# An earlier last conversion, smaller attention buffers and two more prefetched weight quarters

## The chip, the cores and the metric

The kernel runs on one core of one Trainium2 chip. The metric is the device time of one execution in microseconds (us). Three runs of the kernel before took 621.95, 622.92 and 623.33 us, so the median is 622.92 us. The profiled execution took 622.67 us, of which 620.7 us lie between its first and its last instruction.

## What is computed

Three layers follow one another, all in float32 precision; the last layer's two weight matrices arrive as float64 words, which the kernel converts to float32 on the chip.

```python
# attention: 4 batches x 12 heads, 448 positions, head size 64
scores = cap * tanh(q @ k.T / sqrt(64) / cap)
x = (exp(scores - max) / (sum + 1e-9)) @ v             # -> x: 1792 tokens x 768

# soft mixture of 8 experts with 4 slots each
logits = x @ phi                                       # 1792 x 32
slot_in = softmax_over_tokens(logits).T @ x            # 32 x 768
for e in range(8):                                     # each expert sees its own 4 slots
    slot_out[e] = relu(slot_in[e] @ w1[e]) @ w2[e]     # w1: 768x1024, w2: 1024x768
x = softmax_over_slots(logits) @ slot_out

# MLP: w_in 768x2048, w_out 2048x768
h = x @ w_in
out = (max(h, 0) + alpha * min(h, 0)) @ w_out
```

## The kernel before

**Attention.** Two heads make a pair, and there are 24 pairs. One loop runs over steps g; pair i has the four steps 4i to 4i+3. The keys of a pair are cut into four chunks that are taken in the order 0, 3, 1, 2. Chunks 0, 1 and 2 hold 128 keys of both heads, so their tile P is 128 x 896 numbers; chunk 3 is the last-key tile: the remaining 64 keys of both heads, 128 x 448 numbers. In a step `qk` (line 365) issues the score matmuls of one chunk, then ScalarE (ACT) takes tanh (line 380) and exp (line 381) of them into a tile P. Two steps later `pv` (line 384) multiplies that tile with v. GpSimd (POOL) adds the P tiles into `acc`: at chunk 1 the sum of chunks 0 and 1 (line 396) and the two halves of the last-key tile (line 400, two instructions), at chunk 2 the third chunk (line 403). Two steps after that, `row_sums` (line 409, tile `rs`) sums `acc` over the keys with TensorE (PE). In the last pair only line 396 runs on POOL, and `row_sums` is called directly in the last step and reads the other tiles itself.

P has four buffers for all chunks, and `acc` two: one for even pairs (pool `acc0`) and one for odd pairs (pool `acc1`). PE's instructions in attention are chained in the written order (line 281); the other engines' order comes from a scheduler that takes the written order and swaps neighbours by its own estimate of when each is ready. Each engine then runs its queue in order.

**Conversion of w_in in the background.** w_in comes in 24 pieces. `conv_w_in` (lines 667 and 176 to 191) turns one piece into float32: one ACT instruction (abs, line 178) and four VectorE (DVE) instructions (lines 179, 183, 186, 189). `store_w_in`, two steps later, writes it to memory and loads the piece after next. `cv_at` (line 663) gives the step of piece n: 4, 6, then 4n+1, so the second step of each pair; the last is step 93, in pair 23. The pieces pass through `cvbuf`, which is slot 10 of the weight slots; it is freed with the last store, at step 95.

**Weights.** There are eleven weight slots of 1.57 MB (`NA`), and expert weights come in halves of that size: w1 of expert 0 in two, w2 in two, and so on. During attention `LOADS` (line 55) names the pairs at whose fourth step the next half is loaded, if a slot is free; the ten slots 0 to 9 are loaded in the pairs 2 to 20, slot 10 in pair 23. Of the twelfth half one quarter (393 KB) is loaded ahead (`load_early`, line 116, `QE` = 1) in pair 21. After attention seven more slots (`NX`) lie in the memory that the attention pools leave; they are loaded in 27 quarters, in address order (line 111), and each waits for the attention tiles under it. All loads go through one queue, SP's, in order. The pools lie one behind the other in the order of lines 232 to 246: nat0, nat1 (4096 bytes a partition each), stk0 (7680), vn0 (1792), acc0 (3584), stk1 (7680), pt (14336) and on. The first quarters therefore lie over nat0, nat1 and stk0, the sixth and seventh reach into acc0.

**Experts and MLP.** PE goes through the eight experts (w1, then w2); when a half has been used, its slot takes the next load (`done_with`, line 171). The MLP follows on the same queue with the converted w_in and with w_out.

Of the kernel before, what the change touches and what calls it, by code (L numbers as in the profile page):

```python
# [8 lines left out]
F32 = mybir.dt.float32  # L9
# [15 lines left out]
def tile_attention_soft_moe_mlp(ctx, tc, q, k, v, cap, phi, w1, w2, w_in, w_out, alpha, out):  # L25
    nc = tc.nc
    B, H, S, D = q.shape
    J = 4
# [4 lines left out]
    NSLOT = phi.shape[1]  # L33
# [8 lines left out]
    SLOT = 3072  # L42
    NA = 11
    NX = 7
    QE = 1
    JK = 3
    KEYS = 128 * JK
    TAIL = S - KEYS
# [3 lines left out]
    LAG = 2  # L52

    CHUNKS = (0, 3, 1, 2)
    LOADS = (2, 4, 6, 8, 10, 12, 14, 16, 18, 20, 22, 23)

    EH = 5
    TBS = (4, 2, 2, 2, 2, 2)
# [16 lines left out]
    xslots = []  # L75
    early = [arena.tile([128, SLOT // 4], F32, tag=f"early{c}", name="w") for c in range(QE)]

# [19 lines left out]
    def may_load():  # L97
        if nload[0] == len(loads):
            return None
        late = loads[nload[0]][0] in ("wi", "wo")  # L100
        fit = [n for n in free if not late or n < NA]
        return fit[0] if len(fit) > (late and kept[0] < NWO) else None
# [124 lines left out]
    def attention():  # L227
        with ExitStack() as pools:
            def pool(name, bufs=1, **kw):
                return pools.enter_context(tc.tile_pool(name=name, bufs=bufs, **kw))  # L230

            nat_0 = pool("nat0")
            nat_1 = pool("nat1")
            stk_0 = pool("stk0")
            v_0 = pool("vn0")
            acc_0 = pool("acc0")
            stk_1 = pool("stk1")
            pt_p = pool("pt", 4)
            v_1 = pool("vn1")
            acc_1 = pool("acc1")  # L240
            ac0_p = pool("aconst0")
            xn_p = pool("xn", 7)
            xu_p = pool("xu", 4)
# [1 line left out]
            sm_p = pool("sm")  # L245
# [2 lines left out]
            ps_a = pool("ps_a", 3, space=PSUM)  # L248
            ps_o = pool("ps_o", space=PSUM)

            nat_p, stk_p, v_p, acc_p = (nat_0, nat_1), (stk_0, stk_1), (v_0, v_1), (acc_0, acc_1)
            stackI = ac_p.tile([128, 128], F32, name="stackI")
            sel = ac0_p.tile([128, GP, 2, 2, 64], F32R, name="sel")
            hot = ac0_p.tile([128, 64], F32, name="hot")
# [3 lines left out]
            phi_rep = ac_p.tile([128, 128], F32, name="phi_rep")  # L258
            z_run = ac_p.tile([128, 1], F32, name="z_run")

            def head(u):
                return slice(64 * u, 64 * u + 64)
# [6 lines left out]
            nat, stk, sc_t, pt, acc, ov, xu, xn = {}, {}, {}, {}, {}, {}, {}, {}  # L269
# [7 lines left out]
            def matmul(*a, **kw):  # L277
                ins = nc.tensor.matmul(*a, **kw)  # L278
                if order:
                    if order[0] is not None:  # L280
                        tc.add_manual_dep(ins.ins, order[0].ins.name, NOSYNC, reason="tilings together")
                    order[0] = ins
                return ins
# [5 lines left out]
            def later(d, fn, *a):  # L289
                bg.setdefault(now[0] + d, []).append((fn, a))  # L290
# [74 lines left out]
            def qk(i, c):  # L365

                kh, kl = stk["k", i]
                qh, ql = stk["q", i]
                ps = ps_s.tile([128, 2, 512], F32, tag="s", name="s")
                for n, (a, b) in enumerate(((kh, qh), (kh, ql), (kl, qh))):  # L370
                    flags = dict(start=(n == 0), stop=(n == 2))
                    if c == JK:
                        matmul(ps[:, 0, :S], a[:, KEYS:], b, **flags)
                        continue
                    for u in range(2):
                        o = 128 * c
                        matmul(ps[:, u, :S], a[head(u), o:o + 128], b[head(u)], **flags)
                n = 1 if c == JK else 2
                pe = pt_p.tile([128, n, S], F32, tag="p", name="p")
                nc.scalar.activation(out=pe, in_=ps[:, :n, :S], func=AF.Tanh)  # L380
                nc.scalar.activation(out=pe, in_=pe, func=AF.Exp, scale=cap_sb)  # L381
                pt[i, c] = pe

            def pv(i, c):
                if c == 0:
                    ov[i] = ps_o.tile([128, 512], F32, tag="o", name="o")
                    acc[i] = acc_p[i % 2].tile([128, 2, S], F32, tag="acc", name="acc")
                o, a, t, pe = ov[i], acc[i], nat["v", i], pt[i, c]
                if i == NPAIR - 1 and c == 2:
                    row_sums(i)  # L390
                for u in range(2):
                    r = slice(TAIL * u, TAIL * u + TAIL)
                    lhsT, rhs = (t[r, 2 * JK, :], pe[r, 0, :]) if c == JK else (t[:, JK * u + c, :], pe[:, u, :])
                    matmul(o[64 * u:64 * u + 64, :S], lhsT, rhs, start=(c == 0), stop=(c == 2))
                if c == 1:
                    nc.gpsimd.tensor_add(out=a, in0=pt[i, 0], in1=pe)  # L396
                    for u in range(2):
                        r = slice(TAIL * u, TAIL * u + TAIL)
                        if i < NPAIR - 1:
                            nc.gpsimd.tensor_add(out=a[r, u, :], in0=a[r, u, :], in1=pt[i, JK][r, 0, :])  # L400
                if c == 2:
                    if i < NPAIR - 1:
                        nc.gpsimd.tensor_add(out=a, in0=a, in1=pe)  # L403
                    xu[i] = xu_p.tile([128, J * 128], F32, tag="xu", name="xu")[:, :S]
                    nc.scalar.activation(out=xu[i], in_=o[:, :S], func=AF.Copy)  # L405
                    if i < NPAIR - 1:
                        later(2, row_sums, i)
# [252 lines left out]

            ncv = KD * (DFF // 512)

            def cv_at(n):

                return J + 2 * n if n < 2 else J * n + 1

            def conv_w_in(i):
                fb, kk = divmod(i, KD)
                t = cvbuf[:, 2, i % 2 * 512:i % 2 * 512 + 512].bitcast(F32)
                to_f32(craw.pop(i), t, (order[0], latest[0]))  # L670
                cout[i] = t
# [30 lines left out]
            for g in range(NPAIR * J + LAG):  # L702
                now[0] = g
                i, c = divmod(g, J)
# [4 lines left out]
                if i < NPAIR:  # L709
                    qk(i, CHUNKS[c])  # L710
                    if c == 1 and i + 1 < NPAIR:
                        trans_k(i + 1)
                        trans_q(i + 1)
                run_bg()
                if i < NPAIR:
                    if c == 0:
                        last = load(i + 2, "kq") or last
                    if c == 2:
                        if i == NPAIR - LAG - 1:
                            load_early(last)  # L720
                    if g == 2:
                        load_w_in(0)
                        load_w_in(1)
                    for n in range(ncv):
                        if cv_at(n) == g - 2:
                            store_w_in(n)
                        if cv_at(n) == g:
                            conv_w_in(n)
                    if c == 3 and i in LOADS and may_load() is not None:
                        load_next(last)  # L730
                if g >= LAG:
                    n, e = divmod(g - LAG, J)
                    pv(n, CHUNKS[e])
                    if e == J - 1:
                        load(n + 2, "v")
# [4 lines left out]

            nc.vector.tensor_scalar(out=z_run, in0=z_run, scalar1=1e-9, scalar2=None, op0=ALU.add)
            nc.vector.reciprocal(out=z_run, in_=z_run)
            diag = sm_p.tile([128, NSLOT], F32, tag="diag", name="diag")
            nc.vector.tensor_scalar(
                out=diag, in0=stackI[:, 0:NSLOT], scalar1=z_run, scalar2=None, op0=ALU.mult
            )
# [10 lines left out]
    def tail():  # L757
# [254 lines left out]
        with (  # L1012
# [3 lines left out]
            with tc.tile_pool(name="ex2", bufs=1, reuse_waits="tile", side="right") as ex2_p:  # L1016
# [6 lines left out]
                with (  # L1023
# [9 lines left out]
                    mlp(ps_w, ps_c, ex_p, cv_p, g_p, ob_p, so, cstk)  # L1033

    attention()
    tail()

# [29 lines left out]
```

## Time and profile before

| | kernel before |
|---|---|
| median of three runs | 622.92 us |
| profiled execution | 622.67 us |
| span of its instructions | 620.7 us |
| attention, to its last matmul | 0 to 274.2 us |
| experts on PE | 274.2 to 349.3 us |
| MLP | 349.3 us to the end |
| busy: PE / DVE / ACT / POOL | 578.6 / 394.7 / 319.3 / 160.1 us |
| moved by DMA | 110.9 MB |

A share of busy time is an average over these three stages, which have different limits, so each stage is read by itself: its waits, and what ends them.

### The profile page before, as it was taken

The numbers are of one execution on the slowest core, as the hardware profiler recorded it, in microseconds if no ns is written. First come the engines' busy times: TensorE is split into PE (matmuls) and PEld (weight loads), VectorE is DVE, ScalarE is ACT, GpSimd is POOL, SyncE is SP. The second block draws the span as 40 slices with busy tenths as digits, with TensorE's granted clock in tenths as the row PEclk, the third lists the DMA queues.
The fourth block names the chain that finished last, engine by engine and source line by source line (L and its number), as shares of the span: only waits on it lengthen the run. The fifth ranks groups of instructions, "written<-read, shape, count | busy, mean of one in ns | idle before, by whom it ended". The sixth has DMA issues, their size and how long they took to land.

```text
span 620.7 us, 10735 instructions
## 1 busy us (share of the span) xinstructions
PE 578.6 (93%) x4110; PEld 384.7 (62%) x4110; DVE 394.7 (64%) x734; ACT 319.3 (51%) x509; POOL 160.1 (26%) x111
## 2 busy tenths in 40 slices
PE   6799898999999999989896899999999999999996
PEld 4344344455445445454452568888888888888886
DVE  4568667696769879640013399999566666666662
ACT  4798898888889687420101266764412121121211
POOL 0668668475848457100000000000000000000000
PEclk9899999999999999979998899999999999999999
DMA  4786897887978661599999999200301001010101
GB/s 103 199 260 158 260 265 214 261 213 210 262 227 265 207 171 53 194 373 370 403 404 407 389 402 408 102 1 1 103 1 51 1 21 32 0 52 2 51 1 51
DMA packets 95169, 110.90 MB, mean 179 GB/s; under 512 B 56208, under 2 KB 70032, under 8 KB 95120
## 3 DMA queue, kind: packets, MB, share of 16 engines
q1 hardware_dynamic: 94976, 110.24, 55.0%
q8 instruction: 32, 0.52, 0.3%
q14 instruction: 17, 0.14, 0.1%
q10 hardware_dynamic: 144, 0.00, 0.0%
HBM read 98.41 MB, written 11.80 MB: 178 GB/s over the span
## 4 chain that ended last, share of the span: by engine, by line
PE 64%; DMA 15%; DVE 8%; ACT 7%; POOL 3%; issue 1%; SPq 1%; ACTq 0%; POOLq 0%
PE oc L941 13%; PE oc L947 13%; PE oc L948 13%; DMA w<-in_moe_w_dram 12%; PE o L278 6%; PE s L278 5%; ACT p L381 2%; PE hps L896 2%; PE aps L870 2%; ACT p L380 2%; DMA q<-in_q_dram 2%; POOL acc L400 2%; PE rs L278 1%; DMA cvbuf<-in_moe_w_in_dram 1%; PE nx L278 1%
## 5 line engine op out<-in xcount | busy, mean ns | idle before, releaser
L947 PE MATMUL oc<-wsp,gh 128*128 128x512 f32 x448 | 151.7, 339 | 0.0
L941 PE MATMUL oc<-wsp,gh 128*128 128x512 f32 x448 | 151.6, 338 | 0.0
L948 PE MATMUL oc<-wsp,gl 128*128 128x512 f32 x448 | 150.7, 337 | 0.0
L912 ACT ACTIVATE gh<-gf 128x256 fp32r<-128x256 f32 (+1 forms) x96 | 43.5, 453 | 133.0 <-DVE gf L911 127.1
L278 PE MATMUL o<-p,v 128*64 128x448 f32 (+1 forms) x384 | 94.0, 568 | 10.1 <-ACT xu L405 10.0
L380 ACT ACTIVATE p<-s 128x896 f32<-128x896 f32 x96 | 79.0, 824 | 28.6 <-PE s L278 19.7
L381 ACT ACTIVATE p<-p,cap 128x896 f32<-128x896 f32 x96 | 91.2, 951 | 2.3
L941 PEld LDWEIGHTS oc<-wsp,gh 128*128 128x128 f32 x448 | 85.0, 190 | 10.7 <-issue 0.9
L948 PEld LDWEIGHTS oc<-wsp,gl 128*128 128x128 f32 x448 | 84.7, 189 | 11.1 <-issue 1.2
L947 PEld LDWEIGHTS oc<-wsp,gh 128*128 128x128 f32 x448 | 85.0, 190 | 9.7 <-issue 0.4
L913 DVE TENSOR_TENSOR gl<-gf,gh 128x256 fp32r<-128x256 f32 (+1 forms) x96 | 45.0, 469 | 45.3 <-ACT gh L912 45.2
L396 POOL TENSOR_TENSOR acc<-p 128x896 f32<-128x896 f32 x24 | 53.0, 2207 | 77.8 <-ACT p L381 77.8
L278 PEld LDWEIGHTS s<-qh,kh 64*128 64x128 f32 (+1 forms) x168 | 18.1, 186 | 67.1 <-ACT p L380 26.1
L400 POOL TENSOR_TENSOR acc<-acc,p 64x448 f32<-64x448 f32 x46 | 54.3, 1180 | 3.1
L908 DVE TENSOR_SCALAR mn<-hps,alpha 128x256 f32<-128x256 f32 (+1 forms) x81 | 39.5, 487 | 23.6 <-PE hps L896 23.5
L403 POOL TENSOR_TENSOR acc<-acc,p 128x896 f32<-128x896 f32 x23 | 49.0, 2129 | 1.8
L278 PE MATMUL s<-qh,kh 64*128 64x448 f32 (+1 forms) x168 | 45.8, 475 | 0.0
L278 PEld LDWEIGHTS o<-p,v 128*64 128x64 f32 (+1 forms) x384 | 19.0, 134 | 34.8 <-ACT xu L405 16.4
L911 DVE SCALAR_TENSOR_TENSOR gf<-hps,mn 128x256 f32<-128x256 f32 (+1 forms) x81 | 34.6, 427 | 2.7
L278 PE MATMUL s<-qh,kl 64*128 64x448 f32 (+1 forms) x168 | 35.5, 367 | 0.0
L278 PE MATMUL s<-ql,kh 64*128 64x448 f32 (+1 forms) x168 | 35.3, 365 | 0.0
L810 PE MATMUL h<-w,slotT 128*32 128x256 f32 x384 | 30.6, 418 | 4.5 <-DMA w<-in_moe_w_dram 4.5
(151 smaller groups left out, 771.6 us busy)
## 6 DMA issues: line engine op xcount, KB each, us to landing
w<-in_moe_w_dram SPq DMA_DIRECT2D x80, 384.0 KB, 8.4
w<-in_moe_w_dram SPq DMA_DIRECT2D x36, 512.0 KB, 8.2
cvbuf<-in_moe_w_in_dram SPq DMA_DIRECT2D x24, 512.0 KB, 4.5
w<-in_moe_w_out_dram SPq DMA_DIRECT2D x16, 768.0 KB, 8.9
w_in<-cvbuf SPq DMA_DIRECT2D x24, 256.0 KB, 2.4
q<-in_q_dram SPq DMA_DIRECT2D x48, 112.0 KB, 4.0
k<-in_k_dram SPq DMA_DIRECT2D x48, 96.0 KB, 5.1
v<-in_v_dram SPq DMA_DIRECT2D x24, 192.0 KB, 3.4
```

The costliest lines, as they stand in the source:

```text
L278: ins = nc.tensor.matmul(*a, **kw)
L380: nc.scalar.activation(out=pe, in_=ps[:, :n, :S], func=AF.Tanh)
L381: nc.scalar.activation(out=pe, in_=pe, func=AF.Exp, scale=cap_sb)
L396: nc.gpsimd.tensor_add(out=a, in0=pt[i, 0], in1=pe)
L400: nc.gpsimd.tensor_add(out=a[r, u, :], in0=a[r, u, :], in1=pt[i, JK][r, 0, :])
L403: nc.gpsimd.tensor_add(out=a, in0=a, in1=pe)
L908: nc.vector.tensor_scalar(out=mn, in0=ps, scalar1=0.0, scalar2=alpha_sb[:, f:f + 1], op0=ALU.min, op1=ALU.mult)
L912: nc.scalar.activation(out=gh, in_=gf, func=AF.Copy)
L913: nc.vector.tensor_sub(out=gl, in0=gf, in1=gh)
L941: ins = nc.tensor.matmul(o, gh[:, ts], wo_h[f][:, cols], start=(f == 0 and not second), stop=False)
L947: nc.tensor.matmul(o, gh[:, ts], wo_l[f][:, cols], start=False, stop=False)
L948: nc.tensor.matmul(o, gl[:, ts], wo_h[f][:, cols], start=False, stop=(f == KF - 1 and not more))
```

## The change

The last piece of w_in is converted at step 85 (pair 21) and not 93. For that the first fourteen pieces come at steps that are mostly three apart, and the ten later ones at the same place in their pair as before, one or two pairs earlier. Slot 10 is freed at step 87, and `LOADS` names pair 21, so slot 10 is loaded there. The last-key tile gets a pool of its own with one buffer of half the size, the other chunks share three buffers, and `acc` has one buffer for all pairs. A small tile of the epilogue (`diag`) is put into memory that is free by then. Three quarters instead of one are loaded ahead (`QE` = 3), and 25 instead of 27 after attention.

```diff
-    QE = 1
+    QE = 3
-    LOADS = (2, 4, 6, 8, 10, 12, 14, 16, 18, 20, 22, 23)
+    LOADS = (2, 4, 6, 8, 10, 12, 14, 16, 18, 20, 21, 22)
-            pt_p = pool("pt", 4)
+            pt_p = pool("pt", 3)
+            ptt_p = pool("ptt")
             v_1 = pool("vn1")
-            acc_1 = pool("acc1")
-                pe = pt_p.tile([128, n, S], F32, tag="p", name="p")
+                pe = (ptt_p if c == JK else pt_p).tile([128, n, S], F32, tag="p", name="p")
-                    acc[i] = acc_p[i % 2].tile([128, 2, S], F32, tag="acc", name="acc")
+                    acc[i] = acc_0.tile([128, 2, S], F32, tag="acc", name="acc")
+            cv_steps = [4, 7, 10, 13, 17, 20, 23, 26, 29, 33, 36, 39, 42, 45]
+            while len(cv_steps) < ncv:
+                cv_steps.append(cv_steps[-1] + J)
             def cv_at(n):
-                return J + 2 * n if n < 2 else J * n + 1
+                return cv_steps[n]
-            diag = sm_p.tile([128, NSLOT], F32, tag="diag", name="diag")
+            diag = phi_rep[:, :NSLOT]
```

## Rows read from the trace of the kernel before

**Rows 1.** The page's slices (40 of 15.5 us): what the DMA engines moved.
```profile
GB/s 103 199 260 158 260 265 214 261 213 210 262 227 265 207 171 53 194 373 370 403 404 407 389 402 408 102 1 1 103 1 51 1 21 32 0 52 2 51 1 51
```

**Rows 2.** Timeline, experts on PE: start us, us, engine, line, out<-in, count [idle <-releaser].
```profile
283.28 2.94 PE L810 MATMUL h<-w,slotT 128*32 128x256 f32 x45
...
290.87 2.94 PE L810 MATMUL h<-w,slotT 128*32 128x256 f32 x45
...
334.45 0.64 PE L810 MATMUL h<-w,slotT 128*32 128x256 f32 x8 [2.65 <-DMA w<-in_moe_w_dram]
...
348.65 0.63 PE L832 MATMUL y<-w,hT 128*32 128x256 f32 x6 [0.40 <-DMA w<-in_moe_w_dram]
```

**Rows 3.** Timeline, pair 3 and the start of pair 4.
```profile
46.34 2.10 POOL L396 TENSOR_TENSOR acc<-p 128x896 f32<-128x896 f32 x1 [2.39 <-ACT p L381]
...
48.51 2.33 POOL L400 TENSOR_TENSOR acc<-acc,p 64x448 f32<-64x448 f32 x2
...
50.30 0.27 PE L278 MATMUL tr<-ident,kt 128*128 128x128 f32 x1
...
50.88 0.54 ACT L380 ACTIVATE p<-s 128x448 f32<-128x448 f32 x1 [0.36 <-POOL acc L400]
...
51.32 0.59 ACT L345 ACTIVATE kh<-tr 128x512 fp32r<-128x512 f32 x1
...
55.20 0.59 PE L278 MATMUL rs<-acc,hot 128*32 128x224 f32 x8
...
55.41 2.35 POOL L396 TENSOR_TENSOR acc<-p 128x896 f32<-128x896 f32 x1 [2.35 <-ACT p L381]
```

**Rows 4.** SP's queue at attention's end, row sums of pair 23, landing times (L111; all weights).
```profile
256.34 6.04 SPq L111 DMA_DIRECT2D w<-in_moe_w_dram  x8
...
256.24 0.59 PE L278 MATMUL rs<-acc,hot 128*32 128x224 f32 x8
...
DMA to landing us min/median/max: 6.5/8.6/9.4
...
DMA to landing us min/median/max: 3.1/8.5/11.2
```

**Rows 5.** Timeline, pairs 11 and 18: first POOL add and row sums of the pair before.
```profile
125.38 2.11 POOL L396 TENSOR_TENSOR acc<-p 128x896 f32<-128x896 f32 x1 [5.51 <-ACT p L381]
...
125.45 0.58 PE L278 MATMUL rs<-acc,hot 128*32 128x224 f32 x8
...
195.44 2.15 POOL L396 TENSOR_TENSOR acc<-p 128x896 f32<-128x896 f32 x1 [2.39 <-ACT p L381]
...
195.69 0.56 PE L278 MATMUL rs<-acc,hot 128*32 128x224 f32 x8
```

**Rows 6.** Timeline, pair 16 to 17, where TensorE is late.
```profile
173.50 2.10 POOL L396 TENSOR_TENSOR acc<-p 128x896 f32<-128x896 f32 x1 [2.36 <-ACT p L381]
...
174.82 0.55 PE L278 MATMUL rs<-acc,hot 128*32 128x224 f32 x4
...
177.17 0.92 ACT L380 ACTIVATE p<-s 128x896 f32<-128x896 f32 x1 [1.71 <-PE s L278]
```

**Rows 7.** Timeline, pair 1: the piece that is converted at step 6.
```profile
27.24 0.41 DVE L179 TENSOR_SCALAR cvbuf<-cvbuf 128x512 f32<-128x512 f32 x1
...
27.52 2.09 POOL L396 TENSOR_TENSOR acc<-p 128x896 f32<-128x896 f32 x1 [3.93 <-ACT p L381]
...
27.69 2.21 DVE L183 TENSOR_SCALAR cvbuf<-cvbuf 128x512 uint32<-128x512 uint32 x1
...
29.69 2.77 POOL L400 TENSOR_TENSOR acc<-acc,p 64x448 f32<-64x448 f32 x2
```

**Rows 8.** Groups by line, whole run: busy us, mean ns | idle before <-releasers.
```profile
L178 ACT ACTIVATE cvbuf<-cvbuf 128x512 f32<-128x512 f32 x24 | 16.1, 672 | 1.7 <-DMA cvbuf<-in_moe_w_in_dram 1.7
```

**Rows 9.** Timeline, pairs 22 and 23.
```profile
242.78 0.58 PE L278 MATMUL rs<-acc,hot 128*32 128x224 f32 x8
...
248.72 0.55 ACT L380 ACTIVATE p<-s 128x448 f32<-128x448 f32 x1 [0.97 <-POOL acc L403]
```

More of the change, by code (lines that the diff above doesn't have):

```diff
@@ L249, in attention @@
             ps_o = pool("ps_o", space=PSUM)
-            nat_p, stk_p, v_p, acc_p = (nat_0, nat_1), (stk_0, stk_1), (v_0, v_1), (acc_0, acc_1)
+            nat_p, stk_p, v_p = (nat_0, nat_1), (stk_0, stk_1), (v_0, v_1)
             stackI = ac_p.tile([128, 128], F32, name="stackI")
```

## The prediction

> **What bounds the kernel now.** I read the page's slices first, then the stages one by one: attention by its timeline and by the waits of the tanh line, the end of attention by the load queue, the experts by TensorE's timeline.
>
> In the slices, DMA moves 171 GB/s in slice 15 (217 to 233 us), 53 in slice 16, 194 in slice 17, and 373 to 408 in the next eight [rows 1]. So the queue idles while attention ends and then runs full through the experts. In the experts TensorE is paced by itself at first: expert 1 begins at 283.28 and expert 2 at 290.87, 7.59 us apart. The last one waits for weights, 2.65 us before its first matmuls and 0.40 before its last ones, which end at 348.65 + 0.63 = 349.28 [rows 2]. That stage ends when the last expert's weights land; the MLP behind it keeps TensorE busy and moves with it.
>
> Attention is bound by a loop over two engines. In pair 3 the first POOL add (line 396) starts at 46.34 and the two half adds end at 48.51 + 2.33 = 50.84. Only then is the last-key tile free; the next pair's tanh of that chunk starts at 50.88, after 0.36 us of idle time that the trace puts down to POOL [rows 3]. ACT then works without a gap until the next first add at 55.41. The loop's period is 55.41 - 46.34 = 9.07 us: 4.54 on POOL, 4.53 on ACT. So POOL has no slack there.
>
> **The change, part by part.** I call d the time by which attention gets longer, and work out first what is won behind it.
>
> *Loads moved ahead.* With the last store at step 87, slot 10 (1.57 MB) and two more quarters (0.79 MB) are loaded in the idle slices. SP's queue is then no longer blocked by a store in the last pair, so the first five quarters, which lie over nat0, nat1 and stk0, go out too, as pair 22 lets go of them (1.97 MB). The sixth reaches into acc0. In the kernel before that was free after pair 22; now pair 23 uses it, and its row sums end at 256.24 + 0.59 = 256.83 [rows 4]. The same weights, the first quarter of the fourteenth half, were the eighth of the 27 quarters before: eight issues end at 256.34 + 6.04 = 262.4, so the eighth goes out at about 262 and, by the median of 8.6 us, lands at 270.5 [rows 4]. Now it goes out at 257.0 + d into an empty queue and lands 3.1 us later (the shortest landing of rows 4), at 260.1 + d. The stream is ahead by 10.4 - d. I take off 0.7: 20 quarters at 393 KB and 404 GB/s [rows 1] take some 20 us, so the stream comes to slot 0 soon after the first expert lets go of it. Gain: 9.7 - d. TensorE's own pace allows a little more: from 283.28, seven experts of 7.59 us and the last matmuls' 0.63 end at 337.0, 12.3 us before 349.28. Were the five early quarters held back, only 2.36 MB / 404 GB/s = 5.8 us would be won; that is the lower end, 10.4 the upper.
>
> *One `acc`.* Line 396 of a pair now has to wait until the row sums of the pair before have read `acc`. In pair 4 they run from 55.20 to 55.79, and the add started at 55.41 [rows 3]: with 0.04 us of signalling (50.88 against 50.84) it is 0.42 us later. Queued behind it on POOL are the half adds and line 403; for the half adds waits the tanh of the last-key chunk, without slack, and behind that ACT's whole queue, which ends again in xu, the scores and the next row sums. So the row sums follow tanh at the same distance, the loop stays closed, and 0.42 is paid in each such pair. I find three kinds:
> - plain pairs whose conversion keeps its place (3, 4, 7, 8, 15): 5 x 0.42 = 2.1 us;
> - pairs 11, 12, 14, 17, 18, in which other matmuls stand ahead of the row sums: the add waits 125.45 + 0.58 + 0.04 - 125.38 = 0.69 in pair 11 and 195.69 + 0.56 + 0.04 - 195.44 = 0.85 in pair 18 [rows 5]; mean 0.74 less their slack, 3.7 us;
> - pairs 13, 16, 19, 20, 21, where the row sums come latest but TensorE is late anyway: in pair 16 the add moves from 173.50 to 175.41, and would end at 177.51, while tanh began at 177.17 after waiting 1.71 for scores [rows 6]. That leaves 0.3 of 1.9; with the half adds up to 0.9. Bounds 0 and 3.9 for the five, I take 1.3, as TensorE's lateness lasts through most of them.
>
> *Conversions at other steps.* The eight pieces at steps 7, 10, 20, 23, 26, 36, 39 and 42 leave the second step, where DVE works on them while POOL idles (2.39 us before line 396 in pair 3). Pair 1 shows a piece at a third step: an instruction that takes as long as line 179's 0.41 takes 2.21, until after the add's end, and the half adds take 2.77 instead of 2.33 [rows 3, 7]. 0.44 more on POOL is 0.44 in the loop. On the other side the abs on ACT (0.67 [rows 8]) then lies outside the stretch from tanh to the row sums, which more than undoes the 0.42. For pairs 1, 2, 5, 6, 9 and 10 this gives from -1.5 us (only the abs counts: 6 x (0.42 - 0.67)) to +6 (0.42 and 0.44 everywhere, and two pieces in pairs 5 and 9). I take 3.0, nearer to pair 1's row, because pairs 5 and 9 have no ACT time to spare for a second piece.
>
> The Trainium skill (SBUF — State Buffer, section "SBUF: two separate sides") calls the port pair of VectorE and GpSimd an exclusive lock, held for the whole instruction. Pair 1's 2.21 us agrees; by that rule every moved piece would meet POOL, and the rival for slower below would be the forecast.
>
> *P's buffers.* Chunks 0, 1, 2 still get a buffer freed by the chunk of the pair before, and the last-key chunk its own, freed by the half adds as in rows 3. In pair 23 it had a buffer that waited for line 403 and started at 248.72 [rows 9]; now line 396 of pair 22 waits for the row sums (242.78 + 0.58 + 0.04 = 243.40) and the half adds end 2.10 + 2.33 + 0.08 later, at 247.91: 0.8 us won. Pairs 22 and 23 also lose their conversions; I count 0.4 more, bounds 0 and 2.
>
> *Nothing.* The other issues on SP (two quarters in pair 21, slot 10 in its fourth step) lie in slices 15 and 16 with the queue mostly empty; if that cover fails, the v load of pair 23 comes late by their landing, 3.1 us. `diag` moves no instruction.
>
> Sum: d = 2.1 + 3.7 + 1.3 + 3.0 - 1.2 = 8.9 us. Gain 9.7 - 8.9 = 0.8 us. The profiled execution took 622.67 (span 620.7 and 2.0 around it), so 621.9; the median of the runs shown is 622.92, and 622.1 from there. I say 622.0 us: two large terms that nearly cancel.
>
> **Rivals.**
> 1. *The row sums' wait is absorbed.* The kh copy on ACT could run in tanh's wait: its transposes end at 50.30 + 0.27 = 50.57, before tanh starts at 50.88, and it stands behind it [rows 3]. If the scheduler puts it ahead, 0.4 us of ACT work leave the loop, and the first two kinds of pairs (5.8 us) cost about 1.3. Then d is 4.4 and the time 617.5. Against: the row shows that it did not swap although swapping would have paid; its estimate of POOL seems too short.
> 2. *Slower: the moved conversions meet POOL.* In pairs 1 to 10 each holds the half adds and the DVE queue, with the qh and kl behind it. Priced at 6 as above and with the loaded pairs at 2.6, d is 13.2 and the time 622.67 + 13.2 - 9.7 = 626.2. It decides once the gain's 9.7 is passed, so if pairs 1 to 10 lose more than 3.8.
> 3. *The change loads less ahead than it seems.* If the five quarters stay behind something in SP's queue, the gain is 5.8 and the time 622.67 + 8.9 - 5.8 = 625.8. Against it: the first eight of them went out within 6 us, with the attention pools still in use for 12 us more [rows 4].
>
> **How the numbers follow.** A run of this kernel can tell 0.2%, 1.2 us, from no change. The forecast has 0.40, with its own range of 619.5 to 624 us: 0.18 of it faster, 0.17 within, 0.05 slower. Rival 1 has 0.26, nearly all faster (0.24, 0.02 within). Rival 2 has 0.25 (0.23 slower, 0.02 within), rival 3 0.09 (0.07 slower, 0.02 within). That makes faster 0.42, same 0.23, slower 0.35. The range takes in rivals 1 and 2 but for their outer parts: 616 to 627.
>
> **What would show it.** The add of line 396 idle until PE's rs and not ACT's p, by 0.4 us in pair 3; plain pairs of 9.5 us instead of 9.07; attention's last matmul near 274.2 + 8.9 = 283; slices 15 and 16 above 150 GB/s; no wait of more than 1 us for weights in the experts, which last about 66 instead of 75 us. The prediction is wrong if plain pairs keep 9.07 us, if pairs 5 and 9 pass 10.5 us, or if the last expert still waits 2 us for its weights.

## The result, and the profile after

The changed kernel takes 630.0 us (median of 4 runs, 628.98 to 631.39), the kernel before 622.94: ratio 1.0107, 95% interval 1.0067 to 1.0148. It is slower by some 7 us, and lies 3.0 us above the top of my range. The profiled execution took 629.46 us, span 627.6. Executions of one kernel can fall into a slower state at a lower granted clock (here two of e2 and one of e6), and all ratios are of the others.

From the page of the changed kernel: what DMA moved in the 40 slices, then the groups of the tanh line and of the first add (busy us, mean ns | idle before, releaser).

```profile
GB/s 105 204 202 159 259 267 182 250 274 213 165 227 240 227 220 185 202 202 368 397 404 405 390 397 404 154 0 2 95 8 50 1 1 52 0 51 2 50 1 50
...
L380 ACT ACTIVATE p<-s 128x896 f32<-128x896 f32 x96 | 79.0, 824 | 38.0 <-POOL acc L396 20.1
...
L396 POOL TENSOR_TENSOR acc<-p 128x896 f32<-128x896 f32 x24 | 51.1, 2127 | 94.5 <-PE rs L278 57.0
```

Slices 15 to 17, which had 171, 53 and 194 [rows 1], now have 220, 185 and 202 (a slice is 15.7 us long here): the queue no longer idles while attention ends. SP's queue shows the loads: slot 10 at 248.03, five quarters at 255.18, and the sixth at 272.35, just after the row sums of pair 23 (271.67 + 0.58 = 272.25), as forecast:

```profile
248.03 1.76 SPq L157 DMA_DIRECT2D w<-in_moe_w_dram  x4
...
255.18 3.21 SPq L111 DMA_DIRECT2D w<-in_moe_w_dram  x5
...
271.67 0.58 PE L278 MATMUL rs<-acc,hot 128*32 128x224 f32 x8
...
272.35 6.46 SPq L111 DMA_DIRECT2D w<-in_moe_w_dram  x10
```

The changed kernel's experts on PE (line numbers are 4 higher than before):

```profile
290.92 3.94 PE L814 MATMUL h<-w,slotT 128*32 128x256 f32 x48
...
299.53 2.94 PE L814 MATMUL h<-w,slotT 128*32 128x256 f32 x45
...
355.83 0.63 PE L836 MATMUL y<-w,hT 128*32 128x256 f32 x6 [0.35 <-DMA w<-in_moe_w_dram]
```

The experts run from 290.92 to 355.83 + 0.63 = 356.46, 65.5 us; before it was 274.16 to 349.28, 75.1 us [rows 2]. So 9.6 us are won there, and attention is 290.92 - 274.16 = 16.8 us longer. The difference, 7.2, is the loss at the experts' end (6.8 at the end of the whole execution). Everything to explain lies in attention. The timeline of pair 3 and the start of pair 4 in the changed kernel (rows 3 has the same place before):

```profile
46.14 0.59 PE L278 MATMUL rs<-acc,hot 128*32 128x224 f32 x8
...
46.83 0.41 DVE L179 TENSOR_SCALAR cvbuf<-cvbuf 128x512 f32<-128x512 f32 x1
46.93 2.27 POOL L396 TENSOR_TENSOR acc<-p 128x896 f32<-128x896 f32 x1 [2.66 <-PE rs L278]
...
47.27 2.22 DVE L183 TENSOR_SCALAR cvbuf<-cvbuf 128x512 uint32<-128x512 uint32 x1
...
49.28 2.75 POOL L400 TENSOR_TENSOR acc<-acc,p 64x448 f32<-64x448 f32 x2
...
49.52 1.51 DVE L186 SCALAR_TENSOR_TENSOR cvbuf<-cvbuf 128x512 uint32<-128x512 uint32 x1
...
51.07 1.51 DVE L189 SCALAR_TENSOR_TENSOR cvbuf<-cvbuf 128x512 uint32<-128x512 uint32 x1
...
52.06 0.55 ACT L380 ACTIVATE p<-s 128x448 f32<-128x448 f32 x1 [0.83 <-POOL acc L400]
...
56.38 0.59 PE L278 MATMUL rs<-acc,hot 128*32 128x224 f32 x8
...
57.17 2.24 POOL L396 TENSOR_TENSOR acc<-p 128x896 f32<-128x896 f32 x1 [2.66 <-PE rs L278]
```

Two things stand there. Line 396 waits for the row sums, as forecast, but starts 0.20 us after they end (46.73 to 46.93), not 0.04. And a conversion now runs beside POOL's adds: its last three instructions take 5.2 us. The pair takes 57.17 - 46.93 = 10.24 us instead of 9.07. In the kernel before, VectorE's conversion ahead of the same add was:

```profile
44.05 0.42 DVE L179 TENSOR_SCALAR cvbuf<-cvbuf 128x512 f32<-128x512 f32 x1
44.51 0.43 DVE L183 TENSOR_SCALAR cvbuf<-cvbuf 128x512 uint32<-128x512 uint32 x1
44.97 0.69 DVE L186 SCALAR_TENSOR_TENSOR cvbuf<-cvbuf 128x512 uint32<-128x512 uint32 x1
45.70 0.69 DVE L189 SCALAR_TENSOR_TENSOR cvbuf<-cvbuf 128x512 uint32<-128x512 uint32 x1
```

The four take 2.3 us and end at 46.39; line 396 starts at 46.34 [rows 3]. The piece at the second step just fitted in front of the add, with nothing to spare. In the changed kernel the piece in pair 3 is the one of step 13, which keeps its step: ACT's abs for it ended at about 43.95 in both kernels, but VectorE came to it at 46.83 instead of 44.05, because the moved piece of step 10 had occupied VectorE from 37.23 to 44.82, beside POOL's adds, and qh, kl and ql were queued behind that.

### The profile page after: what moved, and what is told of

Read it like the earlier page. It is cut to its first block, busy times and chain, and to the rows that moved or that the text cites. A ratio compares the mean times of both kernels' runs of the same rounds, so it can differ in the third digit from the quotient of the medians.

```text
span 627.6 us, 10740 instructions
## 1 busy us (share of the span) xinstructions
PE 576.2 (92%) x4110; PEld 385.2 (61%) x4110; DVE 414.1 (66%) x734; ACT 319.0 (51%) x509; POOL 160.4 (26%) x111
## 4 chain that ended last, share of the span: by engine, by line
PE 57%; DMA 12%; ACT 9%; DVE 9%; POOL 8%; issue 3%; SPq 2%; POOLq 0%; ACTq 0%
PE oc L945 13%; PE oc L951 13%; PE oc L952 13%; DMA w<-in_moe_w_dram 7%; POOL acc L400 4%; POOL acc L396 4%; PE o L278 3%; PE s L278 3%; ACT p L380 3%; ACT p L381 3%; PE hps L900 2%; PE aps L874 2%; DVE cvbuf L186 2%; PE h L814 2%; DMA cvbuf<-in_moe_w_in_dram 1%
## 5 line engine op out<-in xcount | busy, mean ns | idle before, releaser
L396 POOL TENSOR_TENSOR acc<-p 128x896 f32<-128x896 f32 x24 | 51.1, 2127 | 94.5 <-PE rs L278 57.0
L403 POOL TENSOR_TENSOR acc<-acc,p 128x896 f32<-128x896 f32 x23 | 50.5, 2197 | 1.8
L836 PE MATMUL y<-w,hT 128*32 128x256 f32 x384 | 30.6, 382 | 1.6 <-DMA w<-in_moe_w_dram 0.9
```

## The experiments

Attention's end is the start of the first expert on PE; "experts" is from there to their last matmul, both in the profiled execution, whose time stands beside them. So each of these two is one execution's. Attention's end also depends on TensorE's clock there: the last twelve matmuls of attention (tile si) take 2 x 1.49 us in the kernel before and in the changed one, at a granted clock of 0.50, the 1.2 GHz level, and 2 x 0.85 us at 1.00, the 2.4 GHz level, in e2, e6 and e14, which is 1.3 us; why was not tried. Ratios are to runs of the kernel before on the same chip.

| kernel | attention ends | experts | profiled | ratio, 95% interval |
|---|---|---|---|---|
| before | 274.2 | 75.1 | 622.67 | |
| changed | 290.9 | 65.5 | 629.46 | 1.0107 [1.0067, 1.0148] |
| e1 one acc | 286.6 | 73.8 | 633.35 | 1.0141 [1.0096, 1.0186] |
| e2 new steps | 282.0 | 66.9 | 622.28 | 1.0013 [0.9970, 1.0055] |
| e3 changed, old steps | 287.4 | 70.3 | 630.96 | 1.0102 [1.0060, 1.0145] |
| e4 changed, early sums | 290.5 | 65.4 | 629.28 | 1.0053 [1.0019, 1.0087] |
| e5 new steps, no DVE | 274.4 | 64.8 | 612.23 | 0.9834 [0.9792, 0.9876] |
| e6 steps 42, 66 | 277.3 | 66.3 | 617.08 | 0.9900 [0.9873, 0.9927] |
| e7 steps 11, 15 | 287.8 | 65.2 | 626.25 | 1.0027 [1.0002, 1.0051] |
| e8 changed, both | 294.9 | 65.7 | 633.59 | 1.0136 [1.0093, 1.0179] |
| e9 steps 66, 78 | 282.9 | 65.0 | 621.09 | 0.9933 [0.9904, 0.9962] |
| e10 new steps, no adds | 272.4 | 64.7 | 610.46 | one run |
| e11 changed, 66, 78 | 284.8 | 65.2 | 622.93 | 0.9989 [0.9964, 1.0013] |
| e12 early sums | 284.6 | 76.6 | 634.71 | 1.0116 [1.0068, 1.0164] |
| e13 steps 66, 70 | 281.8 | 65.1 | 620.21 | 0.9951 [0.9917, 0.9985] |
| e14 one piece, 66 | 272.1 | 68.5 | 613.51 | 0.9858 [0.9807, 0.9909] |

**e1: the wait alone.**
```diff
-                    acc[i] = acc_p[i % 2].tile([128, 2, S], F32, tag="acc", name="acc")
+                    acc[i] = acc_0.tile([128, 2, S], F32, tag="acc", name="acc")
```


> The kernel before with one acc buffer for all pairs and nothing else changed: the wait of line 396 for the row sums alone, with the conversions in their old places. Attention's last matmul was at 274.2 us in the profiled execution of the kernel before; d is how much later it gets, and nothing is loaded earlier here, so d goes to the end whole. Theory A (the wait on the row sums was priced too low and makes most of the 16.8 us by which attention got longer): at least 12 us of d, a plain pair over 9.9 us instead of 9.07, time 635 us or more. Theory B (the conversions at other steps make the excess, the wait costs what was predicted, 2.1 + 3.7 + 1.3 = 7.1 us): plain pairs of 9.5 us, time about 630 us. Theory C (the wait and the conversions cost much only together, because the late adds of POOL meet the conversions on VectorE that had kept clear of them): less than 6 us here, time 625 to 629 us.

Attention is 12.4 us longer: theory A's size. Timeline of this kernel, pairs 4 and 5, row sums and first add:

```profile
57.70 0.58 PE L278 MATMUL rs<-acc,hot 128*32 128x224 f32 x8
...
58.48 2.46 POOL L396 TENSOR_TENSOR acc<-p 128x896 f32<-128x896 f32 x1 [2.97 <-PE rs L278]
...
67.72 0.59 PE L278 MATMUL rs<-acc,hot 128*32 128x224 f32 x8
...
68.51 2.11 POOL L396 TENSOR_TENSOR acc<-p 128x896 f32<-128x896 f32 x1 [2.96 <-PE rs L278]
```

The add starts 0.20 us after the sums each time. Without such a stretched add as at 58.48, a pair takes 9.68 us instead of 9.07 to 9.11, so 0.6: the 0.38 of overlap in rows 3 (55.79 - 55.41) and 0.20 of signalling. Most conversions of the second step still end before the add here (67.30 + 0.69 = 67.99 in pair 5), as POOL comes later too. The time is 2 us below theory A's, as the experts are 1.3 us shorter.

**e2: the conversions and loads alone** (`cv_steps` as in the change).
```diff
-LOADS = (2, 4, 6, 8, 10, 12, 14, 16, 18, 20, 22, 23)
+LOADS = (2, 4, 6, 8, 10, 12, 14, 16, 18, 20, 21, 22)
-                return J + 2 * n if n < 2 else J * n + 1
+                return cv_steps[n]
```


> The kernel before with the new conversion steps and load pairs alone (two acc buffers, P's four buffers, one early quarter). Slot 10 and five quarters go out early, so about 8 to 9.7 us are won in the experts. Theory A: attention gets longer by the 3.0 us that were predicted for the moved conversions or less, time 616 to 618 us. Theory B: the conversions alone cost 9 us or more of d, time 622 to 625 us. Theory C: d of 1 to 6 us, pairs 1 to 10 longer by less than half of the 11.2 us that they lost in the changed kernel, time 615 to 620 us.

The shift of line 396 against the kernel before is 9.1 us by pair 11, stays between 8.9 and 9.1 to pair 23, and 1.3 of it come back at attention's end, by the clock of the si matmuls: 7.8. That lies between theories B and C; the time is in B's range. The executions that the ratio rests on go from 622.1 to 628.0 us and the profiled one is the second shortest of them, so 7.8 is from the low end. Two pairs carry most: pair 7 takes 13.53 and pair 10 15.74 us (9.10 and 12.41 before). Timeline of pair 7, with the first and the last instruction of the piece before it in front:

```profile
77.59 1.62 DVE L179 TENSOR_SCALAR cvbuf<-cvbuf 128x512 f32<-128x512 f32 x1
...
84.66 0.68 DVE L189 SCALAR_TENSOR_TENSOR cvbuf<-cvbuf 128x512 uint32<-128x512 uint32 x1
...
87.33 2.08 POOL L396 TENSOR_TENSOR acc<-p 128x896 f32<-128x896 f32 x1 [3.68 <-ACT p L381]
...
87.71 1.99 DVE L179 TENSOR_SCALAR cvbuf<-cvbuf 128x512 f32<-128x512 f32 x1
...
87.82 0.97 PE L278 MATMUL rs<-acc,hot 128*32 128x224 f32 x8
...
89.49 2.48 POOL L400 TENSOR_TENSOR acc<-acc,p 64x448 f32<-64x448 f32 x2
...
89.73 1.25 DVE L183 TENSOR_SCALAR cvbuf<-cvbuf 128x512 uint32<-128x512 uint32 x1
...
91.01 1.51 DVE L186 SCALAR_TENSOR_TENSOR cvbuf<-cvbuf 128x512 uint32<-128x512 uint32 x1
...
92.05 2.42 POOL L403 TENSOR_TENSOR acc<-acc,p 128x896 f32<-128x896 f32 x1
...
92.56 2.47 DVE L189 SCALAR_TENSOR_TENSOR cvbuf<-cvbuf 128x512 uint32<-128x512 uint32 x1
...
94.95 0.44 DVE L430 TENSOR_SCALAR sums<-rs,guard 128x224 f32<-128x224 f32 x1
...
95.44 0.60 PE L278 MATMUL tr<-ident,q 112*128 112x112 f32 x4 [1.98 <-DVE sums L430]
...
97.37 0.54 ACT L405 ACTIVATE xu<-o 128x448 f32<-128x448 f32 x1 [2.66 <-PE o L278]
```

I call this a hit. The piece that is hit is the one of step 29, which keeps its step. Ahead of it the moved piece of step 26 had taken from 77.59 to 85.34 beside the adds of pair 6, so VectorE came to the next piece only as line 396 began. Each of VectorE's instructions then ends 0.3 to 0.6 us after POOL's add of that time, so the piece takes 7.3 us, not 2.3. Line 430, the copy of the row sums out of PSUM, is behind it in VectorE's queue: the sums were ready at 88.79 and are copied at 94.95. TensorE wants that buffer for the transposes of q and stands 1.98 us; ACT stands 2.66 for the matmuls behind them. Then TensorE's granted clock is at 0.61 and 0.54 in the stretches 96 to 98 and 98 to 100 us (half of it would be 0.50, its 1.2 GHz level), and the matmuls that follow are slow as well: the first pair of score matmuls takes 0.74 us at 97.26, 0.47 at 90.04. The Trainium skill (SBUF — State Buffer, section "SBUF: two separate sides") calls the port pair of VectorE and GpSimd an exclusive lock whose loser blocks for the whole instruction; the row of 0.42 us that takes 1.99 agrees.

**e3: the changed kernel without its steps.**
```diff
-                return cv_steps[n]
+                return J + 2 * n if n < 2 else J * n + 1
-LOADS = (2, 4, 6, 8, 10, 12, 14, 16, 18, 20, 21, 22)
+LOADS = (2, 4, 6, 8, 10, 12, 14, 16, 18, 20, 22, 23)
```


> The changed kernel with the old conversion steps and load pairs (one acc, the last-key tile in a pool of its own, three early quarters). The two more quarters save at most 0.79 MB / 404 GB/s = 1.9 us. Theory A: d as in the kernel with one acc alone, 12 us or more, time 633 us or more. Theory B: d of about 7 us, time 628 us. Theory C: below 6 us of d, time 623 to 627 us. If the smaller buffers of P cost something by themselves, this kernel's attention is longer than that of the kernel with one acc alone; I expect less than 1 us either way.

13.2 us of attention, as in e1 (12.4): P's smaller buffers cost under 1 us. By the last line 396 both shifts are 12.6 and 12.7. The time is 3 us below theory A's, as 3.5 instead of 1.9 us were won in the experts against e1.

**e4: row sums a step earlier.**
```diff
-                        later(2, row_sums, i)
+                        later(1, row_sums, i)
```


> The changed kernel with the row sums written one step earlier (in the first instead of the second step of the next pair), so that TensorE sums acc about two us before line 396 wants it; everything else as changed. Theory A: the wait goes and with it 12 us or more of d, time 614 to 618 us. Theory B: the conversions stay and so does most of d, time 624 us or more. Theory C: without the late adds VectorE's conversions at the second step fall into POOL's idle time again; only the pieces moved to third and fourth steps still meet POOL, d of 2 to 6 us, time 615 to 620 us. The line 396 should be idle until ACT's p again and not until PE's rs; if the row sums are held by line 403 of the pair before, TensorE waits there instead and this experiment tells less.

(In steps of the loop, the sums of a pair move from the fourth to the third step of the next one.) Line 396 does not wait for the sums any more. The runs spread from 622.8 to 630.8 us, and in the profiled one, near the upper end, attention is only 0.4 us shorter than in the changed kernel. By these numbers it is theory B's case, theories A and C missed. But this does not show that the wait was cheap: pairs 5 and 10 take 14.9 and 16.8 us, so the remedy for one wait made others. e12 takes that up.

**e5: without VectorE's part of the moved pieces** (on top of e2's edit; "..." marks what is left out here).
```diff
         first = nc.scalar.activation(out=t, in_=hi.bitcast(F32), func=AF.Abs, scale=65536.0)
+        if not dve:
...
+            return
...
+                to_f32(craw.pop(i), t, (order[0], latest[0]), cv_at(i) not in (7, 10, 20, 23, 26, 36, 39, 42))
```


> The kernel with the new conversion steps and two acc buffers, but the four VectorE instructions of the eight pieces at steps 7, 10, 20, 23, 26, 36, 39 and 42 are left out (those pieces of w_in are only half converted; ACT's abs, the load and the store stay). With them attention ended at 282.0 us, 9.1 us of shift being there by pair 11. Theory D (VectorE's conversion behind POOL's adds: four instructions take 7.2 instead of about 2.3 us, the row sums' copy queues behind them and TensorE, then ACT, behind that): pairs 1 to 11 lose at most 1.5 us instead of 9.1, attention ends at 273 to 275 us, time 613 to 616 us. Theory E (the abs on ACT, the loads and stores at other steps, or the second piece in pairs 5 and 9 as such): at least 5 us of the shift stay, time 618 us or more.

Theory D: attention ends 0.2 us later than before, against 7.8 in e2. So it is VectorE's part; abs, loads and stores at the other steps cost nothing that can be seen.

**e6 and e7: two additional pieces, late or early** (`LOADS` as in e2; e7 has 11 and 15 in place of 42 and 66).
```diff
+            cv_steps = [4, 6, 9, 13, 17, 21, 25, 29, 33, 37, 41, 42, 45, 49, 53, 57, 61, 65, 66, 69, 73, 77, 81, 85]
-                return J + 2 * n if n < 2 else J * n + 1
+                return cv_steps[n]
```


> The kernel before (two acc, four P buffers, one early quarter) with the last piece in pair 21 too, but by only two additional pieces, at the third steps of pairs 10 and 16 (steps 42 and 66), where POOL idles for 5.5 and 6.2 us; all other pieces keep the second step. Theory D: no VectorE conversion meets POOL, attention lengthens by 0 to 2 us less 1.3 at its end, the experts last about 67 us as with the other new steps, time 613 to 617 us: faster than both kernels. Theory E: a second piece in a pair costs about 1 us of ACT and VectorE each wherever it stands, and the earlier queue the rest: 618 to 621 us.

> The same with the two additional pieces at the fourth steps of pairs 2 and 3 (steps 11 and 15), where POOL's adds run. Theory D: each of the two meets POOL and costs 0.4 to 4.4 us, the smallest and the largest loss of a pair with the new steps; the pairs behind them go back to their period of 9.1 us; time 615 to 621 us, above the kernel with the pieces in pairs 10 and 16. Theory E: the same time as that kernel within 1 us.

e6 is faster than both kernels, by 1.0%, but by less than theory D had it: the piece at 66 cost 0.0 by the next pair, the one at 42 a hit of 4.4. The piece at 66 met the adds too and took from 177.37 to 182.78, and yet the pair was not longer. So a stretched piece need not cost anything by itself. Timeline of e6, pair 10:

```profile
116.88 1.25 DVE L183 TENSOR_SCALAR cvbuf<-cvbuf 128x512 uint32<-128x512 uint32 x1
118.17 2.45 DVE L186 SCALAR_TENSOR_TENSOR cvbuf<-cvbuf 128x512 uint32<-128x512 uint32 x1
120.55 0.61 DVE L528 COPY ls<-lg 128x448 f32<-128x448 f32 x1
...
121.21 0.55 PE L278 MATMUL tr<-ident,k 128*128 128x128 f32 x3 [2.74 <-DVE ls L528]
```

I had read POOL's idle time ahead of pair 11's add and placed the piece a pair too early: it began beside the adds of pair 10. e7 falls outside every theory: 13.6 us of attention. Pair 2 lost 4.4 and pair 5, which has no additional piece, 7.0. Besides VectorE two other queues show there, in PE's timeline of pair 5:

```profile
81.07 0.87 PE L278 MATMUL tr<-ident,k 128*128 128x128 f32 x3 [6.82 <-DMA k<-in_k_dram]
```

and in ACT's of pair 2:

```profile
47.48 0.66 ACT L178 ACTIVATE cvbuf<-cvbuf 128x512 f32<-128x512 f32 x1 [2.45 <-DMA cvbuf<-in_moe_w_in_dram]
```

With pieces two steps apart, ACT's abs is due before its piece has landed, and ACT waits in its queue. What made k late the waits of SP's queue say (64 to 73 us: total us, times, longest):

```profile
SPq L676 <- DVE cvbuf L189: 5.4, 1, 5.4
```

Line 676 is the store of a converted piece. It stood in SP's queue until VectorE had ended the stretched piece of step 17 at 69.54, and the loads of k, in order behind it, went out at 72.00. So a stretched conversion reaches TensorE by a second way: store, SP's queue, k. This is read from the rows; no run tried it by itself.

**e8: the changed kernel with both remedies.**
```diff
-                        later(2, row_sums, i)
+                        later(1, row_sums, i)
-            cv_steps = [4, 7, 10, 13, 17, 20, 23, 26, 29, 33, 36, 39, 42, 45]
...
+            cv_steps = [4, 6, 9, 13, 17, 21, 25, 29, 33, 37, 41, 42, 45, 49, 53, 57, 61, 65, 66, 69, 73, 77, 81, 85]
```


> The changed kernel with both suspected causes taken away: row sums written one step earlier, and the two additional pieces at steps 42 and 66. One acc, the small last-key pool and three early quarters stay. If the wait on the row sums (12.4 us alone) and the moved conversions (7.8 us alone) are all that attention lost, its last matmul comes at 274 to 278 us, the experts last 65.5 us, and the time is 613 to 617 us. If the early row sums cost something of their own (their matmuls now stand ahead of scores, which ACT waits for), every pair is longer than 9.1 us and the time is 618 to 624 us.

Wrong: 20.8 us of attention. The early sums cost something of their own, and more than supposed.

**e9: steps 66 and 78** (the kernel before; the rest of the edit as in e6).
```diff
+            cv_steps = [4, 6, 9, 13, 17, 21, 25, 29, 33, 37, 41, 45, 49, 53, 57, 61, 65, 66, 69, 73, 77, 78, 81, 85]
```


> The kernel before (two acc, four P buffers, one early quarter) with the two additional pieces at steps 66 and 78, in pairs 16 and 19, where POOL idles for 6.2 and 6.8 us before the next line 396; all others at the second step of their pair. With the pieces at 42 and 66 the one at 42 held pair 10 up by 4.4 us, the one at 66 cost 0.0 by the next pair. Theory D (only pieces that meet POOL's adds on VectorE cost anything): attention ends 1 us earlier than in the kernel before, the experts last 66 us as in the one with steps 42 and 66, time 611 to 614 us. Theory F (a fourth-step piece costs a pair about 4 us wherever it is and the one at 66 was lucky): 616 to 618 us.

(Steps 42, 66 and 78 are third steps; they are what theory F means.) Theory F's sign, and more: pair 19 took 20.41 us instead of 14.24. The piece at 78 ran behind that of 77 beside the adds of 206.30 to 213.41, line 430 behind it came at 213.89, and TensorE and ACT waited for it. Another 0.9 us went to the piece at 66 and 1.5 were lost behind the last line 396.

**e10: without POOL's adds** of lines 400 and 403 in the first eleven pairs (on top of e2's edit).
```diff
-                        if i < NPAIR - 1:
+                        if 10 < i < NPAIR - 1:
...
-                    if i < NPAIR - 1:
+                    if 10 < i < NPAIR - 1:
```


> The kernel with the new conversion steps and two acc buffers, in which POOL's adds of lines 400 and 403 are left out in pairs 0 to 10 (the sums there cover only chunks 0 and 1; line 396 stays). Look at VectorE's conversions in pairs 6 to 10. Theory D (VectorE waits for POOL's port): the pieces at steps 26 to 42 take 2.3 us for their four instructions, or up to 4 where they meet line 396, instead of 7.2, and no pair from 1 to 10 is longer than 11 us. Theory G (they take long for a reason of their own, such as the raw piece's arrival or ACT's abs): they take 6 us or more as before, and pairs 7 and 10 keep 13.5 and 15.7 us.

Theory D: no pair from 1 to 9 is longer than 10.3 us, and pair 10 takes 12.41 as before. VectorE's time on the pieces (view by stretch, 16 to 135 us, tile cvbuf: length, busy (count), clock, DMA share, GB/s), in turn in the kernel before, e2, e10 and the changed kernel:

```profile
16.00:135.00 119.00, 36.90 (x52) 0.99 0.82 228
```
```profile
16.00:135.00 119.00, 63.31 (x56) 0.93 0.80 227
```
```profile
16.00:135.00 119.00, 39.12 (x60) 0.99 0.86 245
```
```profile
16.00:135.00 119.00, 67.59 (x55) 0.97 0.79 224
```

Per instruction 0.71, 1.13, 0.65 and 1.23 us. With the same steps and without the adds, the stretching is nearly gone: 5 of the 96 instructions take over 1 us, 26 in e2. That removing the adds also gave ACT slack is a reservation for the pairs' length, not for these durations.

**e11: the changed kernel with steps 66 and 78.**
```diff
-            cv_steps = [4, 7, 10, 13, 17, 20, 23, 26, 29, 33, 36, 39, 42, 45]
...
+            cv_steps = [4, 6, 9, 13, 17, 21, 25, 29, 33, 37, 41, 45, 49, 53, 57, 61, 65, 66, 69, 73, 77, 78, 81, 85]
```


> The changed kernel (one acc, row sums where they were, small last-key pool, three early quarters), only with the two additional pieces at steps 66 and 78. If the two causes add up: the wait on the row sums alone, 12.4 us, less the 9.6 us won in the experts: 625 to 627 us, and attention's last matmul at 286 to 287 us instead of 290.9. If the conversions make nearly all of the 16.8 us in the changed kernel: below 620 us. If the wait does: 629 us or more.

10.6 us of attention and no difference in time from before. The first case is the nearest; attention ends at 284.8, 1.2 us earlier than it had, and the median is 624.0. What remains is of the size of the wait (12.4 in e1). Of the 96 instructions with which VectorE converts pieces, 3 take over 1 us here, 9 in the kernel before and 31 in the changed one.

**e12: early sums alone**, in the kernel before.
```diff
-                        later(2, row_sums, i)
+                        later(1, row_sums, i)
```


> The kernel before with the row sums written one step earlier and nothing else changed (two acc, old conversion steps). This prices the remedy that failed: if it costs nothing by itself, 621 to 624 us; if the earlier row sums move VectorE's queue so that the conversions of the second steps meet POOL's adds, pairs of 13 us and more appear as in the changed kernel with early sums, 627 to 640 us.

10.5 us of attention, the second case. Of the 96 conversion instructions 27 take over 1 us. Pair 3 alone takes 16.50; there TensorE waits for k, in its timeline. The rows under it are the wait of SP's queue (37 to 46.5 us) and the loads of k in this kernel and, last, in the kernel before:

```profile
55.19 0.90 PE L278 MATMUL tr<-ident,k 128*128 128x128 f32 x3 [5.64 <-DMA k<-in_k_dram]
```
```profile
SPq L675 <- DVE cvbuf L189: 6.0, 1, 6.0
```
```profile
46.18 1.58 SPq L322 DMA_DIRECT2D k<-in_k_dram  x2
```
```profile
39.44 1.73 SPq L322 DMA_DIRECT2D k<-in_k_dram  x2
```

It is the second way of e7 again: the store waits 6.0 us for VectorE's last conversion instruction, and k goes out 6.7 us later than before. Moving one small group of matmuls by a step changes what VectorE and SP's queue do for a whole pair.

**e13 and e14: what is left** (the kernel before; the rest of the edits as in e6; e13 above, e14 below).
```diff
+            cv_steps = [4, 6, 9, 13, 17, 21, 25, 29, 33, 37, 41, 45, 49, 53, 57, 61, 65, 66, 69, 70, 73, 77, 81, 85]
...
+            cv_steps = [4, 6, 9, 13, 17, 21, 25, 29, 33, 37, 41, 45, 49, 53, 57, 61, 65, 66, 69, 73, 77, 81, 85, 89]
```


> The kernel before with the two additional pieces at steps 66 and 70 (pairs 16 and 17), all others at the second step, last piece at 85. The piece at 78 had begun on VectorE at 208.85 us, behind the piece of step 77 and beside the adds of 206.30 to 213.41, and held the row sums' copy to 213.89: it ran a pair earlier than the gap that I had looked at. Step 70 should run in the gap ahead of line 396 of pair 17, 6.2 us in the kernel before. Theory D (position against the adds decides): at most 1 us lost by pair 18, attention ends about 1 us earlier than before, 611 to 614 us. Theory H (VectorE has no 2.3 us to spare in any pair that has a piece already, so one of them meets the adds): 4 to 6 us lost by pair 18, 616 to 619 us.

> The kernel before with one additional piece, at step 66, which was free, and the last piece at 89 (pair 22) instead of 85 or 93; slot 10 is loaded in pair 22. No piece should meet the adds. Attention ends within 1 us of the kernel before; slot 10 and the five quarters still go out before attention ends, so 7 to 9 us are won in the experts: 613 to 616 us. If the store at step 91 comes in the way of the last pair's loads or of the quarters, less is won: 617 us or more.

e13: theory H by its loss, with the time 1 us above its range; 5.4 us were lost in pairs 17 and 18, where the piece at 70 began at 191.76, behind the gap and beside the adds of lines 400 and 403. The piece at 66 costs 0.8 by pair 17 here, 0.9 in e9 and 0.5 in e14, after 0.0 in e6. e14 is the best of all, ratio 0.9858: its attention has no hit and ends 2.0 us earlier than before, and slot 10 and five quarters still go out in its last pair. The piece at 66 does meet the first add of pair 16, which takes 3.54 us. Of the 2.0 us, 1.3 are the clock of the si matmuls and 0.9 lie in pair 9 (9.49 instead of 10.41), where the edit changes nothing, so I don't count them for it; 6.6 us are won in the experts, a little less than the 7 to 9 expected. Its page's slices, and PE in its experts:

```profile
GB/s 102 200 261 158 263 273 223 254 214 225 250 251 215 215 238 42 312 376 384 402 406 402 388 397 405 22 1 1 104 1 53 0 44 10 0 53 2 51 1 51
```
```profile
272.12 2.80 PE L811 MATMUL h<-w,slotT 128*32 128x256 f32 x48
...
339.94 0.63 PE L833 MATMUL y<-w,hT 128*32 128x256 f32 x6 [0.39 <-DMA w<-in_moe_w_dram]
```

## Why the prediction was wrong

- **The gain in the experts was right**, in size and in its way: 9.6 us against 9.7, the sixth quarter held until the row sums of pair 23 as forecast, the weights' waits down to 0.4 us. Attention failed: 16.8 us against 8.9.
- **"Conversions at other steps", 3.0 us with bounds -1.5 to +6, is the step that failed most**: 9.1 us in e2, outside its bounds. I priced 0.44 us of POOL from pair 1's row and not what stands behind a stretched piece in VectorE's queue. Where that is line 430 or 528, TensorE and ACT stop: pair 7 loses 4.4 and pair 10 3.3 us in e2, pair 10 4.4 in e6, pair 19 6.2 in e9. I had also counted the pieces that keep their step as harmless. A moved piece ahead of them makes VectorE late, they have nothing to spare before the add, and the largest hit of e2 (step 29) and the stretched piece in pair 3 of the changed kernel (step 13) are such pieces.
- **The wait on the row sums was right in its place and mis-sized**: 12.4 us in e1 against 2.1 + 3.7 + 1.3 = 7.1. By e1's shifts: plain pairs 3.8 instead of 2.1, the pairs 11, 12, 14, 17 and 18 5.5 instead of 3.7, PE-late pairs 1.2 (1.3 forecast); pairs 0 to 2, 5, 6, 9 and 10, which I had priced with the conversions or, pair 0, not at all, 3.3; pair 22 and the end -1.3. One number that failed is the 0.04 us of signalling, taken from a POOL-to-ACT row: from TensorE to POOL it is 0.20. In the ten pairs of the first two kinds that makes 1.6 of the 3.5 us by which they exceed the forecast. Pair 15 alone has 1.9, and pair 16 behind it gives 0.8 back; the rest was not taken apart.
- **The end** (-1.2) measured -1.3 in e2, and that is luck: the 1.3 us there are the si matmuls at the faster clock (2 x 0.85 instead of 2 x 1.49 us), and e2 has P's four old buffers, while most of the term was to come from the new ones. From line 396 of pair 22 to attention's end the changed kernel is 1.4 us shorter than before, but e1, with the old buffers and all its conversions, is so too (1.35). No run shows a gain from P's buffers.
- **Together** the two parts cost 16.8 and not 12.4 + 7.8 = 20.2. Of the 3.4 between, 2.5 lie in the pairs 0 to 10, where both are at work, and 2.1 in the pairs 20 and 21, which take 12.02 and 10.81 us in the changed kernel and 13.55 and 11.40 in e1; at the end 1.2 go the other way, by e2's clock. That a pair late by one part is partly covered for the other is my guess. With the single terms this closes: 5.3 too little for the wait, 6.0 for the conversions and the end, less 3.4, is the 7.9 us by which attention was longer than forecast.
- **Rivals.** The second, moved conversions meeting POOL, named the cause of the larger miss; its 13.2 us of attention was still 3.6 short. The first (the kh copy goes ahead) did not happen, nor did the third: five quarters went out at 255.18, 36 us before attention's end. Of the signs, the wait on PE's rs came (57.0 us in the group's row), "pairs 5 and 9 pass 10.5" came (11.43 and 10.85), which I had named as the mark of a wrong prediction; attention ended 8 us later than the 283 forecast.
- **The rule that I had set aside** (the Trainium skill, SBUF — State Buffer, section "SBUF: two separate sides") spoke against this change: an exclusive lock of VectorE and GpSimd. The rows above bear it out.

## What to carry over

Before moving background work, look at what it ends against now: a piece that ends as another engine's next instruction begins has no slack, whatever the busy share says. Price a stretched instruction by the queues behind it, its own engine's and, where a store waits for it, the load queue's, to the engine that then stands, and take a signalling time from a row of the same two engines. And take the smallest edit that buys the early load: one additional piece, at a step where it cost 0.5 us (e14), gave -1.4%, where eight pieces off their second step and a shared buffer gave +1.1%.

## What was unexpected in the hardware

A wait of TensorE-to-POOL ended 0.20 us after the matmuls' recorded end in e1, POOL-to-ACT 0.04 us after the add's [rows 3]. The conversions' in-place instructions are stretched beside POOL's adds from 0.42 to as much as 2.26 us (changed kernel) and from 0.69 to 2.57 (kernel before), and the adds from 2.33 to 2.75 (both halves), 2.11 to 2.42 and, the first add of pair 16 in e14, 2.10 to 3.54; line 434, which reads PSUM, took 0.38 us beside the add at 52.10 in the changed kernel and was not stretched. TensorE's granted clock was 0.61 and 0.54 in the 4 us after its stand of 2 us in e2's pair 7, with score matmuls of 0.74 instead of 0.47 us, so a hit costs more than the stand itself.
